# Moving the ones product of the first attention behind the next pair's scores, with one add-up less and one more step of weights beside it

## The chip, the cores and the metric

The kernel runs on one core of a Trainium2 chip. The time is the device time of the core in microseconds (us). Most executions of a kernel agree within 0.3 %. A profile is one execution, and its span lies about 1.8 us below the time of the same run. The profiled run of the kernel before took 1404.63 us, more than each of its timed runs below. The engines are TensorE (PE, its weight loads PEld), VectorE (DVE), ScalarE (ACT), GpSimd (POOL) and SyncE (SP), which issues most transfers.

## The reference

Attention with RMS-normalised q and k, over 8 batches, 12 heads, 448 tokens and 64 dimensions, then two large products, all in fp32:

```python
q_n = q / np.sqrt(np.mean(q*q, -1, keepdims=True) + 1e-06) * g_q      # k_n likewise
scores = np.matmul(q_n, k_n.transpose(0, 1, 3, 2)) / np.sqrt(64)
attn = np.exp(scores - np.max(scores, -1, keepdims=True))
attn = attn / (np.sum(attn, -1, keepdims=True) + 1e-09)
x = np.matmul(attn, v)                # (8,12,448,64) -> x of (3584, 768)
h = np.maximum(x @ w_in, 0.0)         # w_in  (768, 2048)
out = (h * h) @ w_out                 # w_out (2048, 768)
```

## The kernel before

The kernel takes the batches two at a time: an attention, a first product (w_in) and a second product (w_out), the next attention being hidden in the second product. The very first attention has nothing to hide in. It works through twelve pairs of heads one after the other. Beside it GpSimd, VectorE and ScalarE already prepare the weights, in four ticks for each step of one block, and the first product starts when it is done.

For each pair, PE computes four chunks of scores and, with the probabilities as input, the values. The sum of each row of probabilities comes from two engines: VectorE adds chunks up (`add_up`), and PE multiplies the sum and the chunks not yet added by a matrix of ones (`total_of`, in the profile `tot`). The transposes of the next pair's k and q lie between. Line numbers of the profile belong to these parts, comments added here (`NAT` is the number of pairs, 12; `NJ` the number of chunks, 4):

```python
def transpose(i, s, n):                        # L737 PE (pt)
    pt = bank("pt", n)                         # n picks a bank of PSUM
    for j in range(NJ):
        nc.tensor.transpose(pt[:, j * SP:(j + 1) * SP], normed[i][s][:, j * P:(j + 1) * P], ident[:SP, :SP])
    if s:
        nc.scalar.copy(qkT[:, i % 2, s], pt)   # L739 ACT, k
    else:                                      # L741 ACT, q with the gains
        nc.scalar.activation(qkT[:, i % 2, s], pt, AF.Copy, scale=gains[:, 0:1])
...
def add_up(i, c):                              # L764 DVE
    acc = acc_of(i)[:SP]
    nc.vector.tensor_tensor(acc, probs[i, 0] if c == 1 else acc, probs[i, c], ALU.add)
...
def total_of(i):                               # L815 PE (tot)
    tots[i] = ps_o.tile([P, S], F32, tag="t", name="tot")
    parts = [acc_of(i)[:SP]] + [probs[i, c] for c in range(2 if i + 1 == NAT else 3, NJ)]
    for n, pr in enumerate(parts):
        for h in range(2):
            nc.tensor.matmul(tots[i][h * D:(h + 1) * D, :], sums["ones"], pr[:, h, :], ...)
...
def attention_alone():                         # one turn of i is one pair
    for i in range(NAT):
        more = i + 1 < NAT
        scores(i, 0)                           # L749 PE (sc), L754 ACT exp
        scores(i, 1)
        ...                                    # i == 0 apart
        if more:
            transpose(i + 1, 1, 0)             # next pair's k, bank 0
        if i + 3 < NAT:
            load(i + 3)
        values(i - 1, (2, 3))                  # L805 PE (pav)
        total_of(i - 1)
        add_up(i, 1)
        if i + 2 < NAT:
            norm(i + 2)                        # L693 ACT, L694/L695 DVE, L697/L699 POOL
        ...
        yield                                  # weights' ticks go in at each yield
        if more:
            transpose(i + 1, 0, 0)             # next pair's q, bank 0 again
        finish(i - 1)                          # L828 to L835 DVE, needs tot
        load_v(i + 1)
        yield
        scores(i, 2)
        scores(i, 3)
        values(i, (0, 1))
        yield
        if more:
            add_up(i, 2)
        combine_x(i - 1)                       # L845 to L850 DVE
        ...
        yield
...
EARLY = 4 * 12                                 # ticks of weights within this attention
for u, _ in enumerate(attention_alone()):
    weights(min(EARLY, 4 + (EARLY - 4) * u // (4 * NAT - 7)))   # L563/L569 POOL, L588/L593/L598 DVE, L575/L591 ACT
```

Both transposes of a pair use bank 0, so the one for q must wait until ScalarE has copied the one for k out (L739). And it needs the q that GpSimd normalises (L699).

Of the kernel before, what the change touches and what calls it, by code (L numbers as in the profile page):

```python
# [310 lines left out]
def load_q(nc, qk, q, i):  # L311

    _, H, S, D = q.shape
    b, h0 = divmod(2 * i, H)
    nc.sync.dma_start(places_of(qk, i, 0)[:S // 4, 0].rearrange("p (h e) -> p h e", h=2),
                      q[b, h0:h0 + 2].rearrange("h (p j) d -> p h (j d)", j=4))


def load_k(nc, qk, k, i):

    _, H, S, D = k.shape
    b, h0 = divmod(2 * i, H)
    dst = places_of(qk, i, 0)[:S // 4, 1].rearrange("p (j h d) -> p j h d", j=4, h=2)
    for h in range(2):
        nc.sync.dma_start(dst[:, :, h], k[b, h0 + h].rearrange("(p j) d -> p j d", j=4))
# [61 lines left out]
def attention_then_ffn_bounded(  # L387
# [41 lines left out]
    NJ = 4  # L429
    SP = S // NJ  # L430
    NPAIR = H // 2
    NFC = DFF // P
# [6 lines left out]
    NAT = 2 * NPAIR  # L439
# [16 lines left out]
    def bank(name, n=None):  # L456

        turn[0] += n is None
        return ps_m.tile([P, S], F32, tag="mn"[turn[0] % 2 if n is None else n], name=name)
# [22 lines left out]
    HW = HC * P  # L482
    WORDS, BLOCKS, EXPS = 7, 2, 4

    EARLY, ALL = 4 * 12, 4 * (2 * NFC + 3)
    assert DM == NW and BLOCKS * 8 * HW + EXPS * NW + 2 * NW <= 3 * HF * S and 2 * NW <= 4 * S and HF % 4 == 0


# [162 lines left out]
    vs, probs, pavs, tots, normed, rstds = {}, {}, {}, {}, {}, {0: rstd0}  # L651
# [3 lines left out]
    def load(i):  # L655
        if i < NAT:
            load_q(nc, qk, q, i)
            load_k(nc, qk, k, i)
            return

        b, h0 = i // NPAIR, 2 * (i % NPAIR)
        for s, src in enumerate((q, k)):
            dst = by_squares(i, 0)[:, s]
            for n in range(4):
                nc.sync.dma_start(dst[n * 32:(n + 1) * 32],
                                  src[b, h0 + n // 2, :, n % 2 * 32:n % 2 * 32 + 32]
                                  .rearrange("(g t) e -> t g e", t=32))

    def by_squares(i, work):
        n = i % 2 * 4 + 2 * work  # L670
        flat = qk[:, n:n + 2].rearrange("p n e -> p (n e)")[:, 0:2 * S]
        return flat.rearrange("p (s g e) -> p s g e", s=2, e=32)
# [11 lines left out]
    def norm(i):  # L684
        if i >= NAT:
            squares(i)
            return norm_by_squares(i)
        raw, sq = (places_of(qk, i, n)[:SP] for n in range(2))
        rstd = rstds[i] = small.tile([SP, 2, 2 * NJ], F32, tag="rstd", name="rstd", bufs=4)
        normed[i] = sq[:, 0], raw[:, 1]  # L690
        if i <= 2:
            return normalise_in_turn(nc, raw, sq, rstd, mhalf)
        nc.scalar.activation(sq, raw, AF.Square)  # L693
        nc.vector.tensor_reduce(rstd, sq.rearrange("p s (n d) -> p s n d", d=D), AX, ALU.add)  # L694
        nc.vector.tensor_scalar(rstd, rstd, 1.0 / D, 1e-6, ALU.mult, ALU.add)  # L695
        flat = rstd.rearrange("p s n -> p (s n)")
        nc.gpsimd.tensor_tensor(flat, flat, mhalf[:SP, 0:4 * NJ], ALU.pow)  # L697

        nc.gpsimd.tensor_tensor(sq[:, 0].rearrange("p (j h d) -> p h j d", j=NJ, h=2),  # L699
                                raw[:, 0].rearrange("p (h j d) -> p h j d", j=NJ, h=2),  # L700
                                rstd[:, 0].rearrange("p (h j) -> p h j ()", h=2).to_broadcast([SP, 2, NJ, D]),
                                ALU.mult)
# [30 lines left out]
    def transpose(i, s, n):  # L733

        pt = bank("pt", n)
# [3 lines that stand above are left out]
            nc.scalar.copy(qkT[:, i % 2, s], pt)  # L739
        else:  # L740
            nc.scalar.activation(qkT[:, i % 2, s], pt, AF.Copy, scale=gains[:, 0:1])  # L741

    def scores(i, c):

        at = i % 2 if i < NAT else 0
        sc = ps_s.tile([SP, 2, 512], F32, tag="s", name="sc")
        for h in range(2):
            rows = slice(h * D, (h + 1) * D)
            nc.tensor.matmul(sc[:, h, 0:S], qkT[rows, at, 1, c * SP:(c + 1) * SP], qkT[rows, at, 0, :],  # L749
                             start=True, stop=True)  # L750
        pr = probs[i, c] = places[(NJ * i + c) % len(places)][:SP]
        if i < NAT:
            for h in range(2):
                nc.scalar.activation(pr[:, h], sc[:, h, 0:S], AF.Exp, scale=rstds[i][:, 1, 2 * c + h:2 * c + h + 1])  # L754
        else:
            nc.scalar.activation(pr, sc[:, :, 0:S], AF.Exp)  # L756

    def acc_of(i):
        return sums[i % 2] if i < NAT else sums["acc"]

    def add_up(i, c):

        acc = acc_of(i)[:SP]
        nc.vector.tensor_tensor(acc, probs[i, 0] if c == 1 else acc, probs[i, c], ALU.add)  # L764
# [35 lines left out]
    def values(i, chunks=range(NJ)):  # L800
        if 0 in chunks:
            pavs[i] = ps_o.tile([P, S], F32, tag="o", name="pav") if i >= NAT or i % 2 == 0 else bank("pav", 1)
        for c in chunks:
            for h in range(2):
                nc.tensor.matmul(pavs[i][h * D:(h + 1) * D, :], vs[i][:, h, c, :], probs[i, c][:, h, :],  # L805
                                 start=(c == 0), stop=(c == NJ - 1))

    def total_of(i):


        tots[i] = ps_o.tile([P, S], F32, tag="t", name="tot")
        parts = [acc_of(i)[:SP]] + [probs[i, c] for c in range(2 if i + 1 == NAT else 3, NJ)]
        for n, pr in enumerate(parts):
            for h in range(2):
                nc.tensor.matmul(tots[i][h * D:(h + 1) * D, :], sums["ones"], pr[:, h, :],  # L815
                                 start=(n == 0), stop=(n + 1 == len(parts)))

    def finish(i):

        b, hp = divmod(i, NPAIR)  # L820
        pav, factors = pavs.pop(i), xT[:, b % 2, hp]
        x = factors
        if i < NAT:


            turned, factors = sums["turned"], sums["factors"]
            few = small.tile([P, S // 32], F32, tag="few", name="few", bufs=1)
            nc.vector.transpose(turned, tots.pop(i))  # L828
            nc.vector.reciprocal(few, turned.rearrange("p (g r) -> p g r", r=32)[:, :, 0])
            nc.vector.transpose(factors.rearrange("p (g r) -> p g r", r=32),  # L830
                                few.rearrange("p g -> p g ()").to_broadcast([P, S // 32, 32]))

            x = x.rearrange("d (p j) -> d j p", j=NJ)
            pav, factors = (t.rearrange("d (j p) -> d j p", j=NJ) for t in (pav, factors))
        nc.vector.tensor_tensor(x, pav, factors, ALU.mult)  # L835
        del vs[i]
# [15 lines left out]
    def attention_alone():  # L852


        for i in range(NAT):
            more = i + 1 < NAT
            scores(i, 0)
            scores(i, 1)
            if i == 0:

                transpose(1, 1, 1)
                scores(0, 2)
                scores(0, 3)
                transpose(1, 0, 0)
                add_up(0, 1)
                add_up(0, 2)
                norm(2)
                load_v(1)
                values(0, (0, 1))
                load(3)  # L870
                yield
                continue
            if more:
                transpose(i + 1, 1, 0)
            if i + 3 < NAT:
                load(i + 3)
            values(i - 1, (2, 3))
            total_of(i - 1)
            add_up(i, 1)
            if i + 2 < NAT:  # L880
                norm(i + 2)
            elif not more:
                norm(NAT)
                load(NAT + 2)
            yield
            if more:
                transpose(i + 1, 0, 0)
            finish(i - 1)
            load_v(i + 1)
            yield  # L890
            scores(i, 2)
            scores(i, 3)
            values(i, (0, 1))
            yield
            if more:
                add_up(i, 2)
            combine_x(i - 1)
            if NAT <= i + 3 < NAT + 2:
                load(i + 3)
            yield  # L900
        values(i, (2, 3))
        total_of(i)
        finish(i)
        combine_x(i)
# [212 lines left out]
    for span in range(NSPAN):  # L1117
        more = span + 1 < NSPAN
# [108 lines left out]
```

## Time and profile before

| | before |
|---|---|
| time, median of 3 runs | 1402.11 us (1399.25 to 1402.9) |
| span of the profiled run | 1402.8 us |
| start of the first product (first `pa`) | 134.48 us |
| first product, to the first scores behind it | 131.83 us |
| all behind that | 1136.5 us |

PE is busy for 98 % of the span. The first attention is the stretch with gaps. The prediction shows the lines for this: a window for each pair, PE's timeline of one pair, and the waits. The table is read from the top down: the change can act only on the first 266 us, and mostly on the first 134.

### The profile page before, as it was taken

Reading aid. Unit: us, or ns where it says so; the run is one execution under the profiler, and the core shown is the slowest. Engines: PE = TensorE matmul, PEld = TensorE weight load, DVE = VectorE, ACT = ScalarE, POOL = GpSimd, SP = SyncE. Lnnn points to the kernel's source line nnn. Section 1 sums busy time; section 2 is a strip of 40 time slices with the busy share of each in tenths; the row PEclk is TensorE's granted clock in tenths of the full one; section 3 lists DMA queues with packets and bytes.
Section 4 is the critical chain, followed back from the end, with each engine's and each line's share of the span. In section 5 each row is a group of like instructions: output and inputs, shape, how many; then the busy total and the mean of one; then the engine's idle time right before and its main releaser. Section 6 shows DMA issues by size and latency. Waiting matters only on the chain.

```text
span 1402.8 us, 14398 instructions
## 1 busy us (share of the span) xinstructions
PE 1378.1 (98%) x4426; PEld 635.5 (45%) x4426; DVE 814.3 (58%) x1404; ACT 420.3 (30%) x621; POOL 590.7 (42%) x400
## 2 busy tenths in 40 slices
PE   8989999999999999999999999999999999999997
PEld 3333444444444454544444455444444445554553
DVE  6989677589876234476767523457777633332111
ACT  7875555433322011233232011232323201110000
POOL 6998888544452022544353122445445302221000
PEclk9999999999999999999999999999999999999999
DMA  8676998645655333345565332344565343323443
GB/s 239 190 196 168 352 374 316 183 104 119 137 113 120 98 88 87 104 103 122 117 136 122 95 96 85 103 105 105 120 128 107 94 102 86 90 86 103 107 110 70
DMA packets 430914, 188.78 MB, mean 135 GB/s; under 512 B 277484, under 2 KB 428780, under 8 KB 430828
## 3 DMA queue, kind: packets, MB, share of 16 engines
q1 hardware_dynamic: 421228, 179.05, 49.3%
q10 hardware_dynamic: 9472, 8.72, 2.3%
q8 instruction: 37, 0.61, 0.2%
q14 instruction: 49, 0.40, 0.1%
q0 software_dynamic: 128, 0.00, 0.0%
HBM read 154.54 MB, written 33.16 MB: 134 GB/s over the span
## 4 chain that ended last, share of the span: by engine, by line
PE 89%; POOL 3%; DVE 3%; issue 1%; DMA 1%; ACT 1%; POOLq 0%; ACTq 0%
PE ps L1044 37%; PE pc L997 10%; PE pd L997 10%; PE pa L997 10%; PE sc L749 9%; PE pav L805 9%; PE pb L997 5%; DMA sw<-w1s 1%; DVE gT L764 1%; POOL rstd L697 1%; POOL gC L569 1%; POOL qk L699 1%; POOL gC L563 1%; DVE gC L598 0%; PE tot L815 0%
## 5 line engine op out<-in xcount | busy, mean ns | idle before, releaser
L1044 PE MATMUL ps<-gT,sw 128*128 128x448 f32 x768 | 299.2, 542 | 0.8 <-POOL gT L974 0.8
L719 POOL TENSOR_TENSOR half<-half,mhalf 128x28 f32<-128x28 f32 x36 | 173.6, 4824 | 262.3 <-DVE half L718 228.8
L1044 PE MATMUL ps<-gC,sw 128*128 128x448 f32 x576 | 225.2, 542 | 0.0
L974 POOL TENSOR_TENSOR gT<-gT 128x448 f32<-128x448 f32 x96 | 93.5, 976 | 311.9 <-ACT gT L970 311.9
L1044 PEld LDWEIGHTS ps<-gT,sw 128*128 128x128 f32 x768 | 143.9, 190 | 151.0 <-issue 146.5
L756 ACT ACTIVATE pr<-sc 112x896 f32<-112x896 f32 x120 | 104.8, 914 | 293.9 <-PE sc L749 201.7
L749 PE MATMUL sc<-qkT 64*112 64x448 f32 x768 | 171.5, 565 | 1.9 <-ACT gT L754 1.1
L1044 PEld LDWEIGHTS ps<-gC,sw 128*128 128x128 f32 x576 | 108.0, 190 | 112.3 <-issue 111.1
L997 PE MATMUL pa<-xT,sw 128*128 128x448 f32 x384 | 154.9, 539 | 0.5 <-DMA sw<-w1s 0.5
L970 ACT ACTIVATE gT<-gT 128x448 f32<-128x448 f32 x96 | 55.3, 576 | 312.6 <-DVE gT L1012 312.6
L749 PEld LDWEIGHTS sc<-qkT 64*112 64x112 f32 x768 | 61.2, 173 | 99.6 <-issue 81.5
L997 PEld LDWEIGHTS pa<-xT,sw 128*128 128x128 f32 x384 | 72.8, 190 | 72.5 <-issue 71.9
L805 PE MATMUL pav<-pr,vt 112*64 112x448 f32 x480 | 100.2, 547 | 0.0
L721 POOL TENSOR_TENSOR qk<-qk,half 128x448 f32<-128x448 f32 x72 | 84.3, 1191 | 2.8
L997 PE MATMUL pb<-xC,sw 128*128 128x448 f32 x192 | 77.6, 540 | 2.0 <-issue 1.5
L1012 DVE TENSOR_TENSOR gT<-z,pd 128x448 f32<-128x448 f32 x32 | 19.9, 621 | 102.2 <-PE pd L997 102.2
L764 DVE TENSOR_TENSOR acc<-acc,pr 112x896 f32<-112x896 f32 x60 | 68.3, 1138 | 18.4 <-ACT pr L756 15.9
L997 PE MATMUL pd<-xC,sw 128*128 128x448 f32 x192 | 77.5, 540 | 1.4 <-DMA sw<-w1s 1.3
L997 PE MATMUL pd<-xT,sw 128*128 128x448 f32 x192 | 78.0, 542 | 0.0
L997 PE MATMUL pc<-xC,sw 128*128 128x448 f32 x192 | 77.4, 539 | 0.0
L997 PE MATMUL pc<-xT,sw 128*128 128x448 f32 x192 | 77.4, 539 | 0.0
L569 POOL TENSOR_TENSOR gC<-gC 128x384 f32<-128x384 f32 x64 | 72.1, 1146 | 2.5
(120 smaller groups left out, 1565.7 us busy)
## 6 DMA issues: line engine op xcount, KB each, us to landing
sw<-w1s SPq DMA_DIRECT2D x224, 192.0 KB, 2.4
sw<-w2s SPq DMA_DIRECT2D x168, 256.0 KB, 3.3
w1s<-gC SPq DMA_DIRECT2D x8, 1344.0 KB, 7.5
w2s<-gC SPq DMA_DIRECT2D x8, 1344.0 KB, 5.7
out_dram<-osb SPq DMA_DIRECT2D x184, 56.0 KB, 1.9
qk<-in_q_dram SPq DMA_DIRECT2D x144, 56.0 KB, 3.0
qk<-in_k_dram SPq DMA_DIRECT2D x144, 56.0 KB, 2.9
vt<-in_v_dram SPq DMA_DIRECT2D x72, 112.0 KB, 2.9
```

The lines of the kernel that those rows point to most:

```text
L569: nc.gpsimd.tensor_tensor(*[blocks_of(n)[:, i] for i in (dst, x, y)], op)
L719: nc.gpsimd.tensor_tensor(half, half, mhalf, ALU.pow)
L721: nc.gpsimd.tensor_tensor(qkn[:, s], raw[:, s], half[:, s * NG:(s + 1) * NG].rearrange("p g -> p g ()").to_broadcast([P, NG, 32]), ALU.mult)
L749: nc.tensor.matmul(sc[:, h, 0:S], qkT[rows, at, 1, c * SP:(c + 1) * SP], qkT[rows, at, 0, :], start=True, stop=True)
L756: nc.scalar.activation(pr, sc[:, :, 0:S], AF.Exp)
L764: nc.vector.tensor_tensor(acc, probs[i, 0] if c == 1 else acc, probs[i, c], ALU.add)
L805: nc.tensor.matmul(pavs[i][h * D:(h + 1) * D, :], vs[i][:, h, c, :], probs[i, c][:, h, :], start=(c == 0), stop=(c == NJ - 1))
L970: nc.scalar.activation(g, src, AF.Relu)
L974: nc.gpsimd.tensor_tensor(g, g, g, ALU.mult)
L997: nc.tensor.matmul(ps, stream[n + i][:, c], rhs[:, c], start=first and c == 0, stop=c == HC - 1, skip_group_check=not first)
L1012: add(g, x, ps, ALU.add)
L1044: nc.tensor.matmul(ps, stream[n][:, c % 4], rhs_of[i][:, c], start=c == 0, stop=c == HF - 1)
```

## The change

The intent: the ones product waits for VectorE's add-ups in most pairs. So one add-up per pair goes (VectorE sums two chunks; PE's ones product takes the other two as they are), and the ones product moves behind the next pair's last scores, where its input is surely ready. `finish` follows it, the loads of q and k move to the head of the pair, and one more step of weights (four ticks) is put beside the attention.

```diff
-    EARLY, ALL = 4 * 12, 4 * (2 * NFC + 3)
+    EARLY, ALL = 4 * 13, 4 * (2 * NFC + 3)
 ...
-        parts = [acc_of(i)[:SP]] + [probs[i, c] for c in range(2 if i + 1 == NAT else 3, NJ)]
+        parts = [acc_of(i)[:SP]] + [probs[i, c] for c in range(2, NJ)]
 ...
             more = i + 1 < NAT
+            if 0 < i < NAT - 3:
+                load(i + 3)
             scores(i, 0)
 ...
                 add_up(0, 1)
-                add_up(0, 2)
 ...
                 transpose(i + 1, 1, 0)
-            if i + 3 < NAT:
-                load(i + 3)
             values(i - 1, (2, 3))
-            total_of(i - 1)
             add_up(i, 1)
 ...
                 transpose(i + 1, 0, 0)
-            finish(i - 1)
             load_v(i + 1)
             yield
             scores(i, 2)
             scores(i, 3)
+            total_of(i - 1)
             values(i, (0, 1))
+            finish(i - 1)
             yield
-            if more:
-                add_up(i, 2)
             combine_x(i - 1)
```

## The prediction

> **What bounds the kernel now.** I read the page first: the busy shares, then the chain of work that ended last.
>
> ```profile
> span 1402.8 us, 14398 instructions
> ...
> PE 1378.1 (98%) x4426; PEld 635.5 (45%) x4426; DVE 814.3 (58%) x1404; ACT 420.3 (30%) x621; POOL 590.7 (42%) x400
> ...
> PE 89%; POOL 3%; DVE 3%; issue 1%; DMA 1%; ACT 1%; POOLq 0%; ACTq 0%
> ```
>
> TensorE (PE) is busy for all but 24.7 us, and the change touches only the first attention and, through the weights' preparation, the first product behind it. So I cut that stretch at the starts of score blocks, one pair of heads per cut, in the table of busy time by window. In it, column 2 is the length, then each engine's busy time with its count, the clock and the DMA share.
>
> ```profile
> core 0: us, PE busy (x) PEld busy (x) DVE busy (x) ACT busy (x) POOL busy (x), PEclk, DMA share, GB/s
> 16.66:26.46 9.80, 9.33 (x51) 3.60 (x49) 7.41 (x13) 9.80 (x17) 4.24 (x3) 1.00 1.13 311
> 26.46:37.47 11.01, 9.48 (x51) 3.51 (x49) 10.74 (x15) 7.99 (x14) 10.40 (x5) 1.00 0.93 246
> 37.47:87.78 50.31, 47.07 (x243) 17.70 (x241) 45.00 (x54) 39.15 (x65) 48.33 (x31) 1.00 0.67 185
> 87.78:98.02 10.24, 9.74 (x49) 3.42 (x49) 10.07 (x12) 9.25 (x16) 10.16 (x6) 1.00 0.46 140
> 98.02:109.04 11.02, 9.54 (x50) 3.50 (x48) 10.88 (x15) 8.00 (x14) 10.75 (x6) 1.00 1.08 292
> 109.04:122.07 13.03, 10.98 (x50) 3.79 (x49) 12.26 (x17) 8.09 (x14) 12.87 (x9) 0.87 0.24 83
> 122.07:134.48 12.41, 12.41 (x62) 4.37 (x60) 11.75 (x18) 6.06 (x10) 8.59 (x5) 1.00 1.10 258
> 134.48:266.31 131.83, 127.95 (x339) 63.12 (x337) 87.82 (x118) 72.19 (x112) 103.89 (x96) 1.00 0.89 317
> ```
>
> The first attention ends at 134.48 us, when the first product starts. Pairs take 9.8 to 13.0 us each. From 26 us on VectorE (DVE) and GpSimd (POOL) are as full as PE. So three engines are nearly balanced, and work moved from one to another gains little. The timeline of PE gives its own need in the pair that starts at 37.47:
>
> ```profile
> 37.47 1.76 PE L749 MATMUL sc<-qkT 64*112 64x448 f32 x8
> 39.16 0.60 PE L737 MATMUL pt<-ident,qk 112*128 112x112 f32 x4
> 39.69 1.72 PE L805 MATMUL pav<-gT,vt 112*64 112x448 f32 x8
> 41.32 1.72 PE L815 MATMUL tot<-gT,ones 112*64 112x448 f32 x8
> 42.97 0.60 PE L737 MATMUL pt<-ident,qk 112*128 112x112 f32 x4
> 43.51 1.76 PE L749 MATMUL sc<-qkT 64*112 64x448 f32 x8
> ```
>
> From start to start: scores 1.69 twice, transposes 0.53 twice, values 1.65 twice, ones product (tot) 1.65: 9.39 us for a pair, and the next begins at 46.85. Ten such pairs from 16.66 and the last with its tail (12.41, without a gap) make 106.3 us; the stretch takes 117.8. So 11.5 us are gaps or slow clock. The waits of PE between 16.6 and 134.5 us (total, times, longest) name most of them, and the second fence those from 134 to 270:
>
> ```profile
> PE tot L815 <- DVE gT L764: 4.4, 5, 1.5
> PE pt L737 <- POOL qk L699: 2.2, 2, 2.0
> PE sc L749 <- ACT gT L754: 1.1, 1, 1.1
> PE pav L805 <- DMA vt<-in_v_dram: 0.9, 1, 0.9
> PE pt L737 <- ACT qkT L739: 0.5, 1, 0.5
> ```
>
> ```profile
> PE pb L997 <- issue: 1.5, 1, 1.5
> PE pd L997 <- DMA sw<-w1s: 1.3, 1, 1.3
> PE pb L997 <- DVE gT L1012: 0.6, 1, 0.6
> PE pa L997 <- DMA sw<-w1s: 0.5, 1, 0.5
> ```
>
> The ones product waits for the adding up (L764), and the transposes at 105.2 and 116.5 us wait for GpSimd's normalising (L699). The waits are shown net of the pipeline's tail, so their sum (9.1) is below 11.5. In the product only 3.9 us of PE are idle.
>
> **What the Trainium skill says.** "SBUF — State Buffer", section "Who interferes with whom", calls the read and write ports that VectorE and GpSimd share an exclusive lock: a VectorE instruction with two SBUF inputs, or in a two-port mode, and a GpSimd one that reads SBUF take turns, and the later one blocks. The trace agrees: an add-up over 112x896 takes 1.08 us alone (69.29) and two take 3.76 at 39.33, while GpSimd's two adds at 40.28 take 3.70 and elsewhere 1.98 (81.63). "VectorE: DVE Perf Modes", section "The perf-mode tier table", caps an fp32 tensor_tensor at one element per cycle; the formula (N+151)/0.96 GHz in its section on the TRN2 errata gives 1.09 us for 896, as measured. So no cheaper add-up is left; only fewer of them. "TensorE: Matmul & The Clock Gate", Part 1, says an idle PE falls to half clock: the window with the 2 us wait has 0.87.
>
> **The change part by part.**
> 1. *One add-up less for pairs 0 to 10.* That takes 11 instructions of 1.09 us alone off VectorE; at the mean of 1.654 us that the 19 of 27 to 120 us show, it is 18.2 us of busy time. It also frees the shared port: GpSimd loses about 0.8 us to each add-up that meets one of its own operations (1.85 against 1.0 us for an L563 add). Eight or nine of them precede the last normalising, at an estimated two in three that collide: some 5 to 6 us of GpSimd.
> 2. *The ones product takes three parts in place of two.* Four more matmuls at 0.207 us (1.65/8): 0.82 us for each of 11 pairs, 9.0 us. All on the bound engine. PE's pair becomes 10.2 us and its least time 10 x 10.2 + 13.2 = 115.2 us, so the phase cannot end before 131.9. Pairs 3 to 7 of today average 10.06 us; these must get slower.
> 3. *The ones product moves behind the next pair's last scores.* Its add-up then has half a pair of time, and 4.4 us of waits (more with the tail, some 6) go.
> 4. *finish later.* At the tail this helps: the tenth pair's finish and combine (131.38 to 135.8 today) come before the last ones product instead of delaying the last finish at 135.77. The 1.46 us gap before the first pb becomes about 0.9.
> 5. *Loads ahead.* In SyncE's own order nothing stands between the old place and the new, as the jumped-over lines issue no DMA. I expect no gain, except where a needless wait drops out.
> 6. *Four more ticks in the attention.* One further step of weights: four GpSimd operations of 1.0 to 1.4 us (4 to 5.6 us), VectorE 0.55 + 0.55 + 0.95 = 2.1, ScalarE 1.9. For GpSimd that eats what part 1 frees: about three of the four ticks fall before the last normalising. In the product the same work is gone, and a weight store stands less in front of the loads: perhaps 1 us of the 1.8 us of waits on sw.
>
> **The sum.** 11.5 us of gaps before; 6 go with part 3. GpSimd gives the rest: its last normalising ends at 116.5 today; +4.8 (part 6), -5.5 (part 1), -1.5 (waits of its own on the late chain of VectorE) puts it near 114.3. From there PE needs 0.53 + 3 x 1.69 + 4 x 1.65 + 3 x 2.47 = 19.6 us, so the product starts near 133.9; without that wait at 131.9, and I take 133.4, or -1.1. The product gives -1.5. A new small wait (first rival) costs +0.5. Together -2.1 us: 1402.1 - 2.1 = 1400.0.
>
> **Rivals.** (a) *ScalarE's copy of the transposed k becomes the wait.* With tot gone from between, the second transpose, which reuses its PSUM bank, comes 0.53 + 1.65 = 2.2 us after the first. At 98.02 scores start, the first transpose at 99.71, the copy ends at 101.79; the new second transpose would be due at 101.9. That is 0.1 us of slack, and pair 1 already shows this wait (0.5). If ScalarE lags by one weights operation (0.93 us) in most pairs, 5 us are lost: 1404 to 1406. Against it: ScalarE has gaps of 0.5 to 4.4 us per pair today.
> (b) *GpSimd stays the bound and the extra step costs its full 5.6 us.* Then the phase ends at 137 to 138 and the product gives 2 back: 1403 to 1405. For it: GpSimd has been full since 38 us. Against: so was the port, which is relieved.
> (c) *PE alone bounds, with no wait left.* Phase end 131.9, product -2.5: 1397.
>
> **Range and chances.** At best about 5 us and at worst about 5 us are at stake, and runs of the kernel before spread over 3.6 us. I take 1396.5 to 1403.5. Two per cent are 28 us, more than all of PE's idle time, so faster gets 0.01; nothing speaks for 28 us lost: 0.01.
>
> **What would show it.** Right: VectorE's add-ups fall from 23 to 12 and its share drops by about 1 point; tot has 44 more matmuls, in groups of 12; no wait of tot on L764; the first pa starts between 132 and 135; windows of single pairs at 10.2 to 10.6 us from the second on; the SyncE queue in the same order. Wrong: pairs above 11 us with the second transposes waiting for L739 (rival a) or L699 (rival b); a first pa after 136; a product that is not faster by at least 1 us; or a change outside the first 270 us, which I hold to be untouched.

## The result

| | before | after |
|---|---|---|
| time, median of 4 runs | 1401.44 us (1399.25 to 1402.9) | 1404.65 us (1403.9 to 1405.33) |
| span of the profiled run | 1402.8 | 1403.5 |
| first `pa` | 134.48 | 137.30 |
| first product | 131.83 | 130.04 |
| all behind that | 1136.5 | 1136.2 |

The ratio of the times is 1.0024, with a 95 % interval of 1.0007 to 1.0041. A ratio is the mean time of one kernel's fast runs over that of the other's of the same rounds, so it is not quite the ratio of the medians quoted. A second set of rounds (a_again below) gave 1.0006 [0.9993, 1.0019]. So the change costs 0.1 to 0.2 %, or it is barely neutral; it did not gain the 2.1 us that were predicted. The attention got longer by 2.8 us, the product shorter by 1.8, the rest stayed. The 2.8 are too few: in this profile of before the very first scores (8.96 us) ran at a slow clock and took 3.33 us, not 1.76, so that pair 1 began at 16.66, where it begins at 15.57 in the changed kernel and at 15.47 in a second profile of before (b_again). Counted from the start of pair 1 the attention got longer by 3.9 us (117.82 to 121.73).

The page of the changed kernel opens with these lines.

```profile
span 1403.5 us, 14485 instructions
...
PE 1385.2 (99%) x4470; PEld 641.6 (46%) x4470; DVE 798.5 (57%) x1393; ACT 419.8 (30%) x621; POOL 584.6 (42%) x400
```

PE has 44 matmuls more and VectorE 16 us less of work, as intended. A busier PE is no gain in itself: here its share rises with the added matmuls.

The windows of the changed kernel, cut at the starts of pairs, have the same columns as in the prediction: length, then busy time and count of PE, PEld, DVE, ACT and POOL, then the clock and the DMA share.

```profile
15.57:29.24 13.67, 11.72 (x54) 4.53 (x52) 8.94 (x16) 11.35 (x18) 8.94 (x6) 0.88 1.14 299
...
39.25:89.33 50.08, 50.08 (x263) 19.38 (x261) 41.70 (x53) 40.84 (x67) 47.60 (x31) 1.00 0.71 196
89.33:104.56 15.23, 11.56 (x54) 4.61 (x53) 10.51 (x13) 8.02 (x13) 14.99 (x10) 0.89 0.88 263
...
137.30:267.34 130.04, 127.64 (x338) 63.41 (x336) 83.41 (x113) 70.75 (x110) 99.13 (x92) 1.00 0.88 304
```

Five pairs from 39.25 on take 50.08 us, 10.02 each, and PE has no gap at all in them: here the change does what it was made for. (The windows left out, 29.24 to 39.25 and 104.56 to 137.30, have no gap either; the first is one pair of 10.01 us.) But the pair at 15.57 takes 13.67 us and the one at 89.33 takes 15.23, both at a reduced clock (0.88, 0.89). The waits of PE in the attention (16.6 to 134.5 us; total, times, longest) name the two culprits.

```profile
PE pt L737 <- POOL qk L699: 3.7, 1, 3.7
PE pt L737 <- ACT qkT L739: 2.0, 1, 2.0
```

Of the five kinds of wait of before, three are gone: those for the adding up (L764), for the exponentials (L754) and for v. The other two have grown. The wait for L739 stands in pair 1 as it did before, but is 2.0 us and not 0.5; the wait for L699 was 2.2 us at 105.2 and 116.5 and is now 3.7 us at 96.95, in pair 8. There is one in each slow pair. The timeline (start, duration, engine, what, and in brackets the idle time before with its releaser) shows the first of them,

```profile
20.74 0.68 ACT L739 COPY qkT<-pt 128x448 f32<-128x448 f32 x1
...
21.47 0.95 PE L737 MATMUL pt<-ident,qk 112*128 112x112 f32 x4 [1.95 <-ACT qkT L739]
```

and the second.

```profile
91.55 1.72 PE L805 MATMUL pav<-gT,vt 112*64 112x448 f32 x8
...
95.59 1.30 POOL L699 TENSOR_TENSOR qk<-qk,rstd 112x512 f32<-112x512 f32 x1
...
96.95 1.01 PE L737 MATMUL pt<-ident,qk 112*128 112x112 f32 x4 [3.67 <-POOL qk L699]
```

Both times it is the second transpose, the one for q, that stands. In pair 1 PE could go on at 19.45 (the values start at 17.80 and need 1.65 from start to start), but the copy L739 is done only at 21.42. In the pair at 89.33 PE could go on at 93.20, and L699 ends at 96.89. After each stall PE runs at a slow clock for a while: the four transposes take 0.95 and 1.01 us, not 0.60, and the scores behind them 3.05 and 2.83, not 1.76.

What the stalls cost can be summed from the windows: 13.67 less 10.01 and 15.23 less 10.02 are 3.7 and 5.2, together 8.9 us, of which 5.8 are idle time (19.45 to 21.47 and 93.20 to 96.95) and 3.1 the slow clock behind it. Without them the first `pa` would have come at 128.4 by this sum, an estimate. That is six microseconds before that of the old kernel, or five when both are counted from the start of pair 1. So the gain was there, and more than all of it was given back in two places.

### The profile page after: what moved, and what is told of

Its sections match the earlier page's. It is cut to its first block, busy times and chain, and to the rows that moved or that the text cites. A ratio compares the mean times of both kernels' runs of the same rounds, so it can differ in the third digit from the quotient of the medians.

```text
span 1403.5 us, 14485 instructions
## 1 busy us (share of the span) xinstructions
PE 1385.2 (99%) x4470; PEld 641.6 (46%) x4470; DVE 798.5 (57%) x1393; ACT 419.8 (30%) x621; POOL 584.6 (42%) x400
## 4 chain that ended last, share of the span: by engine, by line
PE 91%; POOL 3%; DMA 2%; issue 2%; ACT 1%; SPq 0%; DVE 0%; POOLq 0%; ACTq 0%
PE ps L1041 37%; PE sc L749 10%; PE pd L994 10%; PE pc L994 10%; PE pa L994 10%; PE pav L805 9%; PE pb L994 5%; DMA sw<-w1s 2%; POOL gC L563 1%; POOL rstd L697 1%; PE tot L815 1%; POOL gC L569 1%; ACT gT L754 1%; PE pt L737 0%; PE idle L374 0%
## 5 line engine op out<-in xcount | busy, mean ns | idle before, releaser
L764 DVE TENSOR_TENSOR acc<-acc,pr 112x896 f32<-112x896 f32 x60 | 68.0, 1133 | 19.4 <-ACT pr L756 16.5
L569 POOL TENSOR_TENSOR gC<-gC 128x384 f32<-128x384 f32 x64 | 73.7, 1171 | 2.5
```

The lines of the kernel that those rows point to most:

```text
L569: nc.gpsimd.tensor_tensor(*[blocks_of(n)[:, i] for i in (dst, x, y)], op)
```

## What could be behind the two stalls

**The move.** In the old order the ones product stood between the two transposes of a pair. It was PE's filler while ScalarE copied k out and GpSimd normalised q. Moved away, the second transpose is due earlier, before its inputs are there: by 1.65 us against the kernel before with its eight matmuls, by 2.3 to 2.4 us against an old order with twelve. Then putting the ones product back, with all else kept, must remove both stalls.

**The 13th step.** GpSimd, VectorE and ScalarE have one more step of weights to do beside the attention, and L699 or L739 comes late for that reason. Then twelve steps must mend it, and the step alone must harm the old kernel.

**The pace of the weights.** The step count also decides at which yields the ticks fall. Other starts or places of the ticks should then move the stalls about.

In the expectations, "theory" and "rival" mean what was held when each was written, group by group; the first group still asked after the step and the pace of the weights, the last one after the move. The experiments came in three groups, the first two on one chip, the third on another, so ratios are compared across groups. Medians of the runs of before that they were held against: 1402.47 (9 runs), 1402.71 (10, of which nine are those of group 1) and 1402.67 us (9). Each kernel was timed in five rounds (five or six runs). The outputs are right.

## The experiments

### Group 1: the step of weights, and how far runs scatter

**b_again**, the kernel before, unchanged.

> The kernel before, unchanged, a second time, to learn how much its time and its first attention vary from run to run. Theory 'the profile of before was an unlucky run': its timed median stays near 1401 us and its profiled span is 1 to 4 us below the 1402.8 us of the first profile, with the first product starting (first pa) 1 to 3 us before 134.5 us. Rival 'the profile of before is typical and the timed runs of after are slow elsewhere': first pa again at 134.5 (within 0.5) and span within 0.7 us of 1402.8.

Measured: 1403.1 us, ratio 0.9996 [0.9982, 1.0010]. Its own profile has the first `pa` at 133.74 and a product of 131.88 us; PE waits 4.5 us for L764 and 2.2 for L699. So the first profile of before is typical within 0.7 us; the first `pa` meets neither view, the span (1402.1) meets the rival's. The 0.7 us are less than what the slow start of the first profile (pair 1 at 16.66, not 15.47) explains. Runs of the same kernel scatter over about 4 us (1400.57 to 1404.2), so a single run tells nothing here; the ratio of five rounds tells about 0.14 %.

**a_ticks12**, the changed kernel with twelve steps:

```diff
-    EARLY, ALL = 4 * 13, ...
+    EARLY, ALL = 4 * 12, ...
```

> The changed kernel with 12 steps of weights in the first attention instead of 13; all else as changed. Theory 'the thirteenth step overloads GpSimd near pair 8, and the stall of PE for L699 (3.7 us plus half clock, near 93 us) comes from it': that stall is gone or under 1.5 us, first pa 3 to 5 us earlier than 137.3, product 1 to 2 us longer, whole time 2 to 4 us below the changed kernel, so 1400 to 1402. Rival 'the stall comes from the move of the sums': the stall stays at 3 us or more and the time stays within 1 us of 1404.6.

Measured: 1403.79 us, ratio 1.0005 [0.9991, 1.0019]; first `pa` 135.17, product 130.75. PE's only wait of this kind is the next line.

```profile
PE pt L737 <- ACT qkT L739: 2.5, 1, 2.5
```

The stall on L699 is gone, the one on L739 is not, and the time hardly moves. The theory had the stall right and the time wrong (it said 1400 to 1402 us). The step has a part in the second stall only.

**b_ticks13**, the kernel before with thirteen steps (`EARLY` = 4 * 13, nothing else).

> The kernel before with only the thirteenth step of weights added. If the step alone is the cost: 2 to 4 us slower than before (1403.5 to 1405.5), with PE waiting longer for GpSimd's L699. If the step is harmless by itself (its work leaves the product as it enters the attention): within 1 us of before.

Measured: 1402.75 us, ratio 1.0002 [0.9988, 1.0015]; first `pa` 134.19, product 130.24. The waits in the attention change their places (L699 3.3 us in four waits, transfers of v 2.5, the ones product 1.9 and 1.6, L739 1.3), and their sum is 10.6 us where it was 9.1. The step alone is harmless, so it falls as the main cause.

**a_start1**, the changed kernel with its ticks spread from the first yield on, so that pair 1 has fewer of them beside it:

```diff
-    weights(min(EARLY, 4 + (EARLY - 4) * u // (4 * NAT - 7)))
+    weights(min(EARLY, 1 + (EARLY - 1) * u // (4 * NAT - 7)))
```

> The changed kernel with one tick of weights after the first pair instead of four, and the other three spread over the phase. Theory 'pair 1 stalls (2.0 us for ScalarE's copy L739, and half clock after it, together 3.5 us) because three weights operations of 0.9 us stand ahead of the exponentials on ScalarE': that stall falls below 0.5 us and the first pa comes 2.5 to 3.5 us earlier, if the later stall for L699 does not grow: 1401 to 1402.5. Rival 'GpSimd decides': the three ticks only push GpSimd's queue later, the stall for L699 grows by as much, and the time stays at 1404 to 1405.

Measured: 1404.85 us, ratio 1.0018 [1.0004, 1.0031]; first `pa` 138.40, product 128.15. The wait for L739 shrinks to 0.3 us, but PE now waits 6.1 us for L699 in five pairs. What the ticks leave in one pair they take in others: the stalls move about with the pace of the weights, but no gain follows. Of the two views in the expectation, the rival's was right. In the paces that were tried, the pace decides where the stalls lie, and not whether there are any.

### Group 2: the parts of the change one at a time

**a_again**, the changed kernel, unchanged.

> The changed kernel, unchanged, a second time, on the same chip as the next three. Theory (the change costs 2 to 3 us, from two stalls of PE): ratio to before 1.001 to 1.003, the same two stalls in the profile (2 us for the copy L739 in pair 1, 3 to 4 us for L699 near 93 us), first pa at 137 (within 1). Rival (the first measurement was a chance of the run): ratio below 1.0005, and other stalls.

Measured: 1403.9 us (1401.04 to 1405.89 in 6 runs), ratio 1.0006 [0.9993, 1.0019]; first `pa` 136.63, product 128.44, waits of 2.5 us for L699 and 2.0 for L739. The same two stalls, but a smaller wait for L699 and a smaller slowdown than the theory had; they lie between the two views. The size of the loss stays between 0.06 and 0.24 %, and of these only the first measurement is clear of zero.

**a_late4_12**, twelve steps, with the first four ticks one yield later, which takes them from ahead of pair 1:

```diff
-    weights(min(EARLY, 4 + (EARLY - 4) * u // (4 * NAT - 7)))
+    weights(min(EARLY, 4 + (EARLY - 4) * u // (4 * NAT - 7)) if u else 0)
```

> The changed kernel with 12 steps, and the four first ticks of weights one yield later, behind pair 1's exponentials and the copy L739 on ScalarE. Theory (two stalls with half clock behind them hide the gain of the move): the wait for L739 falls from 2.5 to below 0.5 us, pairs stay at 10.0 us, and first pa comes 3 to 5 us before the 135.2 of the variant with 12 steps, at 130 to 132; time 1399 to 1402, below before. Rival (GpSimd decides whatever PE does): with the first stall gone GpSimd falls behind, waits for L699 of 2 us or more appear, and first pa stays above 133.5 and the time above 1402.

Measured: 1402.35 us, ratio 0.9990 [0.9976, 1.0004]; first `pa` 132.68, product 132.40. The wait for L739 is 1.5 us and has moved to pair 2 (32.45 us); there is none for L699. So both views missed: the stall was not gone, as the theory had it, and GpSimd did not fall behind. The attention is 1.8 us shorter than in the first profile of before (both had the slow start, with pair 1 at 16.59 and 16.66) and the product 0.6 us longer. So later ticks with one step less bring the change level with the kernel before, within the interval, and no further.

**a_two_adds12**, the move alone: twelve steps, both add-ups and the short ones product as before, but the ones product, `finish` and the loads in their new places.

```diff
-    EARLY, ALL = 4 * 13, ...
+    EARLY, ALL = 4 * 12, ...
-        parts = ... range(2, NJ)]
+        parts = ... range(2 if i + 1 == NAT else 3, NJ)]
                 add_up(0, 1)
+                add_up(0, 2)
             yield
+            if more:
+                add_up(i, 2)
             combine_x(i - 1)
```

> The changed kernel with 12 steps but two add-ups and the short ones product as before: the move and the loads alone. If the longer ones product is a pure cost on the bound engine: PE's pair needs 0.8 us less, about 9.2, and first pa comes before 133, time 1399 to 1401. If VectorE and the port it shares with GpSimd are the true bound: pairs take 9.8 to 10.3 us, with new waits of PE for ScalarE or GpSimd, first pa at 134 to 136 and time 1402 to 1404.

Measured: 1407.84 us, ratio 1.0036 [1.0021, 1.0051]; first `pa` 137.96. Of PE's waits in the attention these two are the largest.

```profile
PE pt L737 <- POOL qk L699: 7.7, 5, 3.8
PE pt L737 <- ACT qkT L739: 2.7, 1, 2.7
```

The move alone, at the old amount of work on every engine, makes the same two kinds of wait, and costs 0.36 %, more than either view expected. This speaks for the move as the cause.

**b_three_parts**, one add-up less alone: the old order and twelve steps, with the three-part ones product. The edit is that of a_two_adds12 in reverse, without the step, on the kernel before.

> The kernel before with one add-up less and the three-part ones product, in the old places, 12 steps. If the extra matmuls cost what they take on PE: waits for the add-up L764 shrink (4.5 to below 2 us) but PE gains 9 us of work, so first pa 1 to 3 us later than before, at 135 to 137, time 1403.5 to 1405.5. If relief of VectorE and GpSimd pays for it: first pa within 1 us of 134, time within 1 us of before.

Measured: 1399.73 us, ratio 0.9979 [0.9965, 0.9992]; first `pa` 129.39, product 132.05. PE's waits from 8 us to the first product and a little behind it are now led by these.

```profile
PE pb L994 <- issue: 1.5, 1, 1.5
PE sc L749 <- ACT qkT L383: 0.8, 1, 0.8
PE pav L805 <- DMA vt<-in_v_dram: 0.6, 1, 0.6
```

There is no wait for L764 left, none for L699 and none for L739. Both views had expected a slower kernel. So with one add-up less the ones product does not wait in its old place either, and there was nothing for the move to remove. Two things changed together here: VectorE adds less, and the longer ones product covers the second transpose for 0.7 us more; no run tells them apart.

### Group 3: the move undone, or mended

**b3_13**, the same with thirteen steps: the kernel before with one add-up less, the three-part ones product and the 13th step.

```diff
-    EARLY, ALL = 4 * 12, ...
+    EARLY, ALL = 4 * 13, ...
-        parts = ... range(2 if i + 1 == NAT else 3, NJ)]
+        parts = ... range(2, NJ)]
                 add_up(0, 1)
-                add_up(0, 2)
             yield
-            if more:
-                add_up(i, 2)
             combine_x(i - 1)
```

> The kernel before with one add-up less, the three-part ones product in its old place, and 13 steps: the change without the move of the ones product and of finish. Theory (the move is what costs: it takes 2.4 us of PE work out from between the two transposes of a pair, so that PE reaches the second one before the copy L739 and the normalising L699 are done): no wait for L739 or L699 above 1 us, first pa at 129 to 131, product 1 to 2 us shorter than with 12 steps, time 1398 to 1400.5, about 4 us below the changed kernel. Rival (the thirteenth step overloads GpSimd with either order): waits for L699 of 2 us or more appear, first pa at 133 or later, time 1402 to 1404.

Measured: 1396.72 us (1396.37 to 1398.35), ratio 0.9964 [0.9951, 0.9978]; first `pa` 129.04, product 129.04, span 1394.6. It beats the kernel before by 5 to 6 us (mean and median) and the changed one by more, and is better than the theory expected. Its timeline at the place of the first stall,

```profile
19.35 2.42 PE L815 MATMUL tot<-gT,ones 112*64 112x448 f32 x12
...
20.80 0.60 ACT L739 COPY qkT<-pt 128x448 f32<-128x448 f32 x1
...
21.71 0.60 PE L737 MATMUL pt<-ident,qk 112*128 112x112 f32 x4
```

and of the second:

```profile
90.08 2.42 PE L815 MATMUL tot<-gT,ones 112*64 112x448 f32 x12
...
90.23 1.40 POOL L699 TENSOR_TENSOR qk<-qk,rstd 112x512 f32<-112x512 f32 x1
...
92.43 0.60 PE L737 MATMUL pt<-ident,qk 112*128 112x112 f32 x4
```

These are to be held against the timelines of the changed kernel, in which PE stands idle. In pair 1 ScalarE's copy ends at the same time in both: 20.74 + 0.68 = 21.42 there, 20.80 + 0.60 = 21.40 here. There PE stands idle from 19.45 to 21.47; here it does its ones product from 19.35 to 21.71 and never notices the copy. ScalarE was no faster; PE merely had something to do. (The kernel before agrees: there the copy ends at 22.53, 5.87 us after the start of pair 1, here 5.83 after it, and in the changed kernel 5.85.)

**a_total_back**, the changed kernel with one line moved back; `finish`, the loads and the 13 steps stay as changed:

```diff
             values(i - 1, (2, 3))
+            total_of(i - 1)
             add_up(i, 1)
 ...
             scores(i, 3)
-            total_of(i - 1)
             values(i, (0, 1))
```

> The changed kernel (13 steps, finish late) with only the ones product back in its old place, in front of the second transposes. Theory of the move: waits for L739 and L699 vanish or stay below 1 us in total, first pa 129 to 131 and time 1398 to 1400.5. Rival (the late finish is the cost): the stalls stay, first pa 134 or later, time 1403 or more.

Measured: 1396.95 us (1396.5 to 1400.38), ratio 0.9966 [0.9952, 0.9979]; first `pa` 129.51, product 129.94, a wait for L739 of 0.9 us in pair 1 and none for L699. One line, and the changed kernel is 0.4 to 0.6 % faster, no different from b3_13 within the intervals. This single edit separates the move from the step and the pace, which it leaves as they are. It also shows that the later `finish` neither helps nor harms by itself.

**a_late_q**, the mirror image: the ones product stays in its new place, and the second transpose goes behind it:

```diff
-            if more:
-                transpose(i + 1, 0, 0)
             load_v(i + 1)
 ...
             total_of(i - 1)
+            if more:
+                transpose(i + 1, 0, 0)
             values(i, (0, 1))
```

> The changed kernel with the second transposes moved as well, behind the ones product; the filler stands in front of them again, though in the new place. Theory of the move: the waits for L739 and L699 vanish (below 1 us in total), pairs stay at 10.0 us, first pa 128.4 to 130.5, time 1397.5 to 1400. Rival (the second transposes come too late for the next pair's scores): a new wait of the scores for L741 in each pair, pairs above 10.3 us, first pa at 133 or later.

Measured: 1399.95 us, ratio 0.9982 [0.9968, 0.9995]; first `pa` 131.36, product 130.3. No wait for L739 or L699 is left, as the theory had it, though the first `pa` comes 0.9 us later than it said. A pair takes 10.16 us here, not 10.02, so part of the gain is missing: the ones product from start to start takes 2.41 us, where it takes 2.31 in the changed kernel with the values behind it.

**a_late_q12**, the same with twelve steps.

> The same with 12 steps. If the thirteenth step is worth what leaves the product: first pa within 1 us of the variant with 13, product 1 to 2 us longer, time 0.5 to 2 us above it. If GpSimd is short of time in the attention: first pa 2 us or more earlier than with 13, and time equal or lower.

Measured: 1402.14 us, ratio 0.9998 [0.9985, 1.0012]; first `pa` 131.73, product 131.88. The 13th step is worth 1.6 us in the product here, about as the first view had it.

Not run: the changed kernel with only its loads put back. It compiles to the same lists of instructions and waits on every engine as the changed kernel (only numbers inside names differ), so that part of the change is nothing.

### All together

Ratios to the kernel before, by the place of the ones product, the add-ups and the steps:

| ones product | add-ups | 12 steps | 13 steps |
|---|---|---|---|
| old place | two | 1 (b_again 0.9996) | 1.0002 (b_ticks13) |
| old place | one | 0.9979 (b_three_parts) | 0.9964 (b3_13), 0.9966 (a_total_back) |
| new place | two | 1.0036 (a_two_adds12) | not run |
| new place | one | 1.0005 (a_ticks12) | 1.0024, 1.0006 (the change) |

Down a column the add-up removed is worth 0.21 to 0.38 %. From old place to new the move costs 0.26 to 0.60 % in each of the three comparisons that can be made. The 13th step seems worth 0.15 % with one add-up less in the old place, which is at the edge of the noise (two groups, each ratio known to 0.14 %), and elsewhere in the table nothing, or up to 0.2 % of loss. In the product alone it is worth 0.7 to 3.0 us (a_again's and the change's profiles against a_ticks12, b3_13 against b_three_parts), where two profiles of one kernel differ by 1.6 (130.04 and 128.44).

### What is left of the second stall

The second stall, in pair 8, needs more than the earlier place of the transpose. In b3_13 the second transpose of that pair begins 6.13 us after the pair's first scores (86.30) and L699 ends 5.33 after them. In the changed kernel it is due 3.87 after them (93.20 less 89.33), 2.3 earlier, but L699 also ends later, at 7.56. Taken apart by subtraction, an estimate, 1.5 us of the stall come from the place (5.33 less 3.87) and 2.2 from the later L699 (7.56 less 5.33).

What GpSimd does from the L699 of the pair before to this one is the same in both kernels, seven operations of the weights (L563, L569) and then L697; first the changed kernel, then b3_13.

```profile
82.78 1.86 POOL L563 TENSOR_TENSOR gC<-words,gC 128x384 int32<-128x384 int32 x1
84.72 4.80 POOL L569 TENSOR_TENSOR gC<-gC 128x384 f32<-128x384 f32 x4
89.48 2.78 POOL L563 TENSOR_TENSOR gC<-words,gC 128x384 int32<-128x384 int32 x2
```

```profile
78.79 1.01 POOL L563 TENSOR_TENSOR gC<-words,gC 128x384 int32<-128x384 int32 x1
79.89 5.12 POOL L569 TENSOR_TENSOR gC<-gC 128x384 f32<-128x384 f32 x4
84.97 1.99 POOL L563 TENSOR_TENSOR gC<-words,gC 128x384 int32<-128x384 int32 x2
```

This round takes 14.08 us in the changed kernel (82.81 to 96.89) and 12.80 in b3_13 (78.83 to 91.63); in both, the rounds with four or five such operations before it take 9.5 to 11.5. With twelve steps (before, a_ticks12) no round between two L699 has more than four. So the 13th step comes as one crowded round ahead of pair 8, and this fits a_ticks12, which keeps the first stall and loses the second. a_again has its second stall behind the same round, and in a_start1 two rounds of seven end at 61.23 and 117.87 us, with waits of 1.45 and 1.92 us behind them (and one of 1.99 behind a round of five). A crowded round is not the only way to be late: with both add-ups kept (a_two_adds12) L699 is late behind rounds of four. With the ones product between the transposes the crowded round is covered, in a_total_back only just: L699 ends at 92.66, the transpose starts at 92.72.

The first stall seems to have little part in the second. One pair earlier L699 ends 3.49 us after the first scores in the changed kernel (82.81 less 79.32) and 3.19 in b3_13 (78.83 less 75.64), so that GpSimd stands nearly the same to PE in both. This is read from traces. No run removes the first stall alone at 13 steps with the pace unchanged, and why the three L563 of the crowded round take 4.6 us here and 3.0 there was not tried, so the split of the second stall is argued, not shown.

## Why the prediction was wrong

It said 1400.0 us with a range of 1396.5 to 1403.5; the first rounds gave 1404.65, outside the range.

- **The step that failed is part 3 with its counterparts in the sum**: "4.4 us of waits (more with the tail, some 6) go" was right as far as it goes, and "a new small wait (first rival) costs +0.5" was not small. It was 5.8 us of idle time and 3.1 us of slow clock, 8.9 us in all. The mechanism was seen: rival (a) named the copy L739 and put the slack at 0.1 us in one late pair, but the sum counted it for 0.5 us. Rival (a) at 5 us and rival (b) had the time right, 1404 to 1406 and 1403 to 1405, but neither way of getting there: the waits came in one pair each, not in most pairs (a), and the step alone costs nothing (b, by b_ticks13).
- **What the part overlooked** is how much the moved instruction was hiding. Rival (a) saw that the second transpose loses its cover, but tried the subtraction at one pair (98.02) and for L739 only. The trace of before held the rest. In pair 1 the prediction's own list has PE waiting 0.5 us for L739 with the ones product in between; without the 1.65 us of that product the wait is 2.1 us, an estimate, and 1.95 were measured. And in the very pair that was tried, L699 ends at 105.11, 3.2 us after the 101.9 at which the second transpose would be due. The sum did use L699, but only its last end (116.5, moved to 114.3), from which PE was to need 19.6 us to the first `pa`. In the changed kernel that L699 ends at 115.83 and nothing waits for it: PE, late by its two stalls, comes to the transpose at 118.49.
- **Part 1** was undervalued. The add-ups fell from 23 to 12 as said. One of them less per pair, alone, removes the waits for L764, L699 and L739 together and makes the kernel 0.21 % faster, some 3 us (b_three_parts). The prediction gave the gain of the L764 waits to part 3. The group of add-ups reads 12 with a mean of 1394 ns now:

```profile
L764 DVE TENSOR_TENSOR gT<-gT 112x896 f32<-112x896 f32 x12 | 16.7, 1394 | 3.6 <-ACT gT L754 3.5
```

  The 3.6 us behind the second bar are idle time of VectorE ahead of the add-ups; it waits for ScalarE's exponentials now.
- **Part 2** was oversized. A full pair takes 10.02 us, not 10.2. The twelve matmuls of the ones product take 2.31 us from start to start, where the prediction reckoned 2.47 by scaling eight.
- **Part 4** made no difference that can be seen in the time (a_total_back against b3_13). The gap before the first `pb`, 1.46 us before and forecast at 0.9, is 0.3 in the changed kernel; but with the late `finish` it is 1.5 in a_ticks12 and a_total_back, so the late `finish` alone does not shorten it. **Part 5** was right: the loads' new place does nothing. The order on SyncE did change, though, against what was to be seen: the 13th step shifts the weight stores among the loads.
- **Part 6** was about right where it could be measured. The product was to gain 1.5 us and gained 1.8 (3.4 in a_again), and b3_13 shows 3.0 against b_three_parts (132.05 to 129.04). What it missed is that the four ticks do not spread evenly: most of GpSimd's extra work falls into the round ahead of pair 8.
- **The first `pa`** was predicted at 133.4 and came at 137.30, 3.9 us late; that the product did better by 0.3 us makes up little of it. The rest of the kernel stayed as it was.

## What to carry to other kernels

Before moving an instruction away from a wait, look at what stands behind it on the same engine: it may be the filler that hides the latency of the next one, and that one's inputs have to be checked in every round, not in one. If a change has several parts, find out which one removes the wait: here one add-up less per pair was enough, and the move only cost. And a short stall can be dearer than its idle time, through the slow clock behind it: here 5.8 us of idle time cost 8.9.

## What the Trainium skill lacked or had wrong

- "TensorE: Matmul & The Clock Gate", Part 1, section "What's actually happening", puts the fall to half clock after at least one idle window of about 3.4 us. In these runs gaps of 1.9 to 2.0 us were enough: behind the gap of 1.95 us before 21.47 in the changed kernel a pair's next scores took 3.05 us, not 1.76, and in a_start1 scores behind gaps of 1.92 and 1.99 us took 2.95 and 2.96. Gaps of 1.45 us there and of 1.81 us in a_two_adds12 (107.75) were not followed by a slow clock. The length of a single gap does not settle it: the first scores stand behind 0.77 us in every run and took 3.33 us in the first profile of before, 1.76 in b_again.
- No page has a figure for what the same group of matmuls costs by its neighbours; it belongs to "TensorEngine Tiling (Array Packing)". The twelve matmuls of the ones product take 2.31 us from start to start between scores and values, and 2.41 us between scores and transposes (a_late_q). In the profile the values have the same tile as the ones product (112*64), the scores and transposes another (64*112, 112*128).
- "SBUF — State Buffer", section "Who interferes with whom", was borne out by the trace of before, as the prediction shows; the later runs were not asked about it.
